# A threshold-attention and SwiGLU kernel: six staging buffers for the gate and value weights, another cutting of the score bursts, and a new written order

## The chip, the cores and the metric

The kernel runs on one core of a Trainium2 chip. Its five engines are TensorE (PE, matmuls, with weight loads listed as PEld), VectorE (DVE), ScalarE (ACT), GpSimd (POOL) and SyncE (SP, which here only issues DMAs). The metric is the time of one execution on the device in microseconds (us), as the median of a few runs. One execution was taken with the hardware profiler; the rows quoted here come from it.

## What is computed

The inputs are q, k and v of shape (8 batches, 8 heads, 576 positions, 64), in fp32. First comes an attention that keeps only scores near the row's maximum, then a feed-forward layer with a gate:

```
scores = (1/8) * q @ k^T                       # per batch and head, 576 x 576
keep   = scores >= max(scores, row) - tau      # tau = 0.02
attn   = softmax(where(keep, scores, -1e9)) @ v
x      = attn, heads side by side              # 4608 tokens x 512
xn     = x / sqrt(mean(x*x) + 1e-6) * rms_g
g      = xn @ w_gate                           # 512 x 1536
val    = xn @ w_val                            # 512 x 1536
out    = (g * sigmoid(g) * val) @ w_out        # 1536 x 512, fp32
```

The scores are computed in fp32. The softmax weights, v, xn and the feed-forward weights are used in fp16.

## The kernel before

**Steps.** The 4608 tokens are 36 chunks of 128 rows: four "m" chunks for each batch, and one "v" chunk for each two batches, made of the last 64 rows of both. A chunk has four steps, one for each pair of heads, so there are 144 steps. A step goes through these stages:

- TensorE computes the scores of the step for both heads of a pair (letter S), fp32, into PSUM banks 0, 1, 3 and 4. One S is a *burst*, and `CHOP` (line 1300) says how many steps are in it: kind 'w' is one step in two half-step parts; a number is a count of columns, so 1024 is 1.78 steps of 576 columns and 1536 is 2.67. A burst may begin only when VectorE has read the banks that it writes.
- VectorE reads the scores, scales them by -1/8, copies them into one of three SBUF buffers `ssb` and takes the row's extreme on the way (`ttr`, letter r, line 767). A step that a burst's end cuts is read in two pieces for each head.
- GpSimd adds tau (`nthr`, letter n), which gives the threshold `nth`.
- ScalarE masks with a Prelu of slope 1e30 (letter p, once for each head) and takes exp of both heads (letter x) into `wsb`.
- The weights are transposed: for the first 16 steps on TensorE (letter T) with an evacuation by VectorE, later by a DMA issued on SyncE (letter t on SP).
- TensorE multiplies by v (letter A, once for two steps), and VectorE divides by the sum (letter h).

When a chunk is complete it is squared and summed (ScalarE, S), its factor is made on GpSimd (m), it is scaled to fp16 (GpSimd, N) and transposed into `xnT`.

**Feed-forward.** Two groups of 256 tokens and eight of 512 each go through 12 column blocks of 128: TensorE's gate product G and value product V (each four matmuls), a tanh on ScalarE (t), then on VectorE `silu` (s) and `gate` (g), which leaves an fp16 block in `hf`. There are 24 such blocks. Twelve of them are tiles of their own, and twelve lie in the memory of `stg`, the staging buffer of the weights. The output product O takes six blocks at a time; ScalarE or VectorE moves its result into `osb` and a DMA stores it. The last group is streamed: its output products follow block by block.

**Weights.** `w_gate` and `w_val` come as twelve loads of 512 KB on SyncE's queue (letter i), each into one of `NSTAGE` = 3 fp32 buffers in turn (line 1217), and GpSimd scales each half by rms_g and casts it to fp16 (letter c, 24 casts, line 1229). A load into a buffer waits for the casts out of it. The third buffer first holds rows of q for the first batch. A `gate` that writes one of the twelve blocks in `stg` for the first time waits for all casts (line 1098). `w_out` comes by four DMAs on GpSimd's queue (M).

**Inputs of later batches.** Batches 0 and 1 load q and k (letters d, D, M, m for batch 0, L for batch 1) and are transposed on TensorE (t, q); later ones are loaded in blocks (l), GpSimd swaps half blocks in place (s) and VectorE transposes (t, T, u). v is loaded (O, a, A) and cast on GpSimd (r).

**Order.** What an engine does, and in which order, is written in `ORDER` (lines 43 to 79): one text for each engine, one letter for each operation; for TensorE the digits after a letter are the PSUM banks that it takes. `in_order` (line 127) reads the texts; each engine then works strictly in its order. `COST`, `DMA_NS`, the due times (`prio`) and the gates belong to the planner that made the texts; here they set no order. What does act on the kernel are the texts, `CHOP`, the buffers and the waits that follow from them.

Of the kernel before, what the change touches and what calls it, by code (L numbers as in the profile page):

```python
# [10 lines left out]
FP16 = mybir.dt.float16  # L11
# [3 lines left out]
AX = mybir.AxisListType  # L15

COST = dict(
    s_main=965.0, s_virt=960.0, tr_qk=570.0, tr4=230.0, tr_full=440.0, av_main=300.0, av_virt=370.0, ffn4=215.8, warm=3500.0,
    evac_qk=600.0, evac_qk_act=465.0, evac_half=252.0, evac_kt=330.0, evac_kt_act=252.0, prelu=667.0, exp2=1060.0, exp1=666.0, exp0=590.0,
    mask_d=680.0, mask_g=1810.0, take_g=1420.0, pool_shift=780.0, pool_sq=1280.0, pool_sum=850.0, trw=510.0, evac_w=400.0, evac_wp=900.0, rz=210.0, xmul=341.0, sq=612.0, xn=773.0,  # L20
    pool_tiny=302.0, pool_mean=944.0, pool_dma=880.0, cast_v=620.0, cast_vt=475.0, cast_w=665.0,
    sp=420.0, sp_v=600.0, sp_w=600.0, sp_tr=1300.0, sp_qk=680.0, sp_tl=630.0, sp_qb=600.0, swap=790.0, turn=600.0, turn_t=210.0, turn_q=680.0,
)
DMA_NS = dict(qkb=1750.0, qk=1200.0, tl=600.0, v=870.0, vt=700.0, wt=1700.0, xt=800.0, out=600.0, w=875.0, wo=2000.0)

LETTERS = dict(
    PE={"emit_av/fn": "A", "emit_burst/fn": "S", "emit_ffn/gmm": "G", "emit_ffn/omm": "O", "emit_ffn/vmm": "V",
# [14 lines left out]
)  # L42
ORDER = dict(
    PE=(
        "wt.1:0t3t1t.1:7St6t7St2t5t6ST67t2t5ST65t7Sq67A2T75ST72SA6q72ST65T72SA2T67ST67q25SA6T72ST67x2Sq62A7x5ST75T62ST67A2k5ST67G2V6G7A1V2T65ST67G0V2",
        "G5SV6G7A5V2SG6V2G5V7G6V2Sl67G2V5A6G7SV2G6V5G1O7V6Sx6A0Ox3O6OA7SG6V7G0V3G1V4A6G7V6SG6V7G0V6G3V7G1V2G4V5G6V7SA6G0V3G1V7A4A6SO6A0OSO7OA2SG6A0V7",
        "G3V1G6A2V7SG6V0G3V1G4V6A7A2SG6V7A0O6SG7V0G3A1O.1:7V2SG0V3G1V4G2V5SOA0A3OA5SO6OSG6V0G7V3G1V4G6V2G0V7G5V6SA7A6A0G3V7O6OSG6V0G3A1V4O7A6SG6V0G3",
        "V1A6G4V2A6SOO6OA5SG6V0G3V1G4V6A7SA6G7V0G3V1G4V6A7SG6O7V0OSG6V0O7A3G4A2OSV6G7A0V3G1V6G4V7A2SO6OO7SA6G0V3OG1V4G6V7A2SG6V0A3O7G3V1G4V6A2SOG0V3",
        "O6A7SG7V0G3A7OV1O7SG6V0G3V1A4G6V2A5SOO6OSG6V0G3V1G4V6A2A7SG7V0A3G1V6G4V7A2SO6G0OV5SG6V0A3G1O7A4V6SG6V0G3V1G4V6OSA6O7OA6SO6A0A3OSG7V0G6V3G7V1",
        "G6V4G2V7G5V6SO7G0A3A1A4V2OSG6V0G3O7V1A6SG6V0G3OV1G4V6A2SA6O7OSG6V0G3V1A4G7V6A2SG7V0G3A6O7OSV6G7V0A3G2O1V3G0V6G4OV7G2V0A3G6A7O3V7A6G2OV0O6OO0",  # L50
        "OG3V1G7V4G3V7G2V3G6V2G7V6G5V1O0G3OO7V5G6OO0134V6G2V5OG2OV6G5OOOOV6OOOOOOOOOOOOOOOOO",
    ),
    ACT=(
        "lT.1TT.2TT.1TppTTxTppxppTTxVppxppppxxVppSxppxppxppVxSppppxxpVpxppxpptExtppxSttppxptpxSptpxttppxvtvpptxttppxppxppxppSxppxpptttxptpppxStxtptpp",
        "ttptxppxxtpptxppSxppxppSxppxpppxpxptpxptpxtSppxptppxttpxppSxtppxppppxxtptppxSpxppxtptptxppxppxSpppxpxppxppppxttxSptpttpptxxtppppxxpSptxptpxp",
        "SpxpptxtppptpxxSppxppppxxtSptpptxpxpptxtptppxSpxtppppxpxpxtptppxpSxppptxttpSxppxpppxpxppptxptxSptpxppptpxtptxpxSpptxppxpptpStxpxppxpptxptptp",
        "xSpxppxppppxtxptptppxxptpSxtptpSpxpxpptppxpxpxtptSppxpxpptxtptpxppxppxSppxppxpppSpxpptxpttxtpptxptxpptpppxxpSxtptppSpxxptpptpxtpxSpxpppppxxp",
        "txtpppxtpxStptppxpppxSxpptpxpptpxxttttSSttttttttttttteses",
    ),
    DVE=(  # L60
        "zcR.1RRrrCrrRRrrSRSrrSSrrhSSrrVSSrrhVrrSSSSrrhSSrrSSVrrhSSrrxSSrrhxVrrSSSSrrSShrSSrsvghSSsgrrrsrSsgSrrrrrrshggrrrsgrrrssggrrrrsghrsr.1rsrsgg",
        "grrxTrrehxrrtTethrrrrrrssgsghgsrgru.2u.2rrrsrgrrssggssggusturrrgrhssghrrtrrhrgrTrThrrrrrrrrrheert.1rrrshgrsrghusrurrrrrsggrrssghht.1grrrrsrr",
        "htgTuurrrrsTrgshrgtrrrTrrrrsTrsggsgrrrrrhrhehrrrerrrerrrrrrssrggsrgsstgsggrrrTrhthrrsThueurrrrsghgsTgrrhrrrrrrsrgshrgshgtrrTrrrruehterrurrss",
        "ggsrrgrrhrrrhsrgstgsrrghrrrrrsrguerrtrrrshrgsuherTrtrrrgrsTgrThsrshggrrrrrruerrrthrTsegrusgrhsrgrrrrhrsrgsgsrghrrrrersrgtthTrrrsrhgrsrgTeurr",
        "rrrsrgrsrghshgTrrrrrertuuerrrrsrgsTgtsrhhrurrrrghrssrgsrhgrrrrrrsggertrrrrhssghrtrgrrrrrsurgssgergrrrhrTrruhTtrrrrhherrurrerurstrsTrgrTrsgss",
        "ggsgrrrrrrhhhsggrerrrssgrgrrhrrrrsrsggrsrgherrrrrrehrrrrsrghsrghrsrrrgsrsrghrrerrrrrgrhsgssgsgghsheshggsegsgssegsgsggessesgggssggessggeeE",
    ),
    POOL=(
        "SnnnrrrrnnrnrcncccnmncccncNcncmncNcrnccncMnrrMncrccrccmncMncNnscnsssncMsrmnsNsnsssssnsssnsssnmsNnsssnssnmnnnnrr.2NnnmnNrnmsNnnsssssnrnssssns",
        "ssssnmrnsrNsssnssnsmnsNnsnnnnmr.1nNnnmnNr.1nnrrnssnsrsnssrmsssnsssnr.1NsssnssnmNsnsr.1ssnnsmsnsNnmNnnnnsrrnsssssnnrmNsssnsnssnmsnNrnssssssns",  # L70
        "r.1nmNnsmsNsnnsr.1nnrrnnnnmsNrsnrsnsssmnssNsnssr.1nr.1msssnsnNsssnssssmNnsnnsnnnmnnNsrnnsssnssmsNnrsrnmsssnsNnsnsssrssnsssnsmnssNnnnmnr.1nnn",
        "r.1NrrnmNnnnnmrNrnmNnnnnnmnnnNnmnNnmNmN",
    ),
    SP=(
        "MmMmdOdDdDDAOLDLSLOOLiOiiLiLiLLiioOOo.1oiiAiOililttllttlltltltAtaasstataTttttttTtllttTtlTltltslttltlttttaTttstttAataTtattTTsltltAtllltsltttl",
        "TtlttstaatsTttTtTtaallttlttltsltltstATlltttTtTstatTtasattsatsltltttllTttAlltsTttllttTtstTatttaslttlaatllttTstllAttltTlsttTtttaTsttstttattTst",
        "atTatttTttsTttsttstttttttTtsTsTTsssssss",
    ),
)

# [93 lines left out]
def kernel(  # L174
# [25 lines left out]
    def sb(name, shape, dt=FP32):  # L200
        return konst.tile(shape, dt, tag=name, name=name)
# [8 lines left out]
    wo = sb("wo", [128, NFC, DM], FP16)  # L210
# [40 lines left out]
    NT_ = 3  # L251
    th = [sb(f"th{i}", [128, 512]) for i in range(NT_)]
    sl = [sb(f"sl{i}", [128, 512]) for i in range(NT_)]
    stg = sb("stg", [128, NSTAGE * 1024])
    stage = [stg[:, 1024 * i:1024 * (i + 1)].rearrange("p (e n) -> p e n", e=2) for i in range(NSTAGE)]
    hf = [sb(f"hf{i}", [128, 512], FP16) for i in range(12)]
    hf += [stg.bitcast(FP16)[:, 512 * i:512 * (i + 1)] for i in range(NHF - 12)]
    osb = [sb(f"osb{i}", [128, DM]) for i in range(2)]
    osb += [ssb[i % NSB][:, i // NSB, 0:DM] for i in range(4)]

# [443 lines left out]
    def emit_burst(segs, prio, runs):  # L704
# [10 lines left out]
        for run in runs:  # L715
            def fn(o, run=run):
                for s, lo, hi, at in run:
                    _, whole, quads = info[s]
                    p = steps[s][1]
                    for rows, bb, lhs in quads if no_whole or o.quad else whole:  # L720
                        for h in range(2):
                            hs = HALF[h]
                            nc.tensor.matmul(bank[rows, at[h]:at[h] + hi[h] - lo[h]], lhs(hs), k_of(bb, p, h)[hs, lo[h]:hi[h]],
                                             start=True, stop=True)

            n = sum(hi[0] - lo[0] for _, lo, hi, _ in run)
            met = [b for s, lo, hi, at in run for h in range(2) for b in banks(at[h], hi[h] - lo[h]) if b not in first]
            for b in met:
                first[b] = lead
            lead += 9.0 + per_col * n  # L730
            made.append(add("PE", 9.0 + per_col * n, prio if not made else -600.0, deps + made[-1:], fn, mode=2 if no_whole else 1))
            made[-1].touches = sorted(set(met))
        made[0].claims = sorted((b, 0.0 if TILE else x) for b, x in first.items())
        writers = {}
# [23 lines left out]
        for n_, (s, lo, hi, at) in enumerate(segs):  # L758
# [7 lines left out]
            for h in range(2):  # L766
# [6 lines left out]

                before = [] if head else [ttr_of[s, h]]
                need = max(writers[b] for b in banks(at[h], hi - lo))
                t = ttr_of[s, h] = add("DVE", 75.0 + (hi - lo) / 0.96, s - 1 + TTR_EARLY + 0.001 * h, (made if TILE else made[:need + 1]) + [o_c, held] + before, ttr)
                t.long = len(segs) > 1 and sum(hi_ - lo_ for _, lo_, hi_, _ in segs) > LONG
                t.reads = list(banks(at[h], hi - lo))
                t.opens = [b for b, last in last_use.items() if (last[1] == h and n_ == len(segs) - 1 if TILE else last == (n_, h))]

    stage_use = []
    ssb_user = {}
    last_burst = []

# [261 lines left out]
    def emit_ffn(slot, parts, ready_step, pace, streamed):  # L1046
# [12 lines left out]
        for fc in range(NFC):  # L1059
# [35 lines left out]
            t = add("ACT", n / 1.2 + 49.0, pr - PUSH[0], [g, th_use.get(i)], tanh, src=(g, 0))  # L1095
            s_ = add("DVE", el, pr - push1, [t, sl_use.get(i)], silu, frees=(g, 0))
            th_use[i] = s_
            m_ = add("DVE", el, pr - push1, [s_, vv] + (stage_use if hi >= 12 and hi not in hf_use else []), gate, frees=(vv, 0))
            sl_use[i] = m_
            hs.append((hi, m_))  # L1100
            uses += [g, vv]
# [112 lines left out]
    for c in range(DFF // 512):  # L1214
        for d in range(0, 4, 2):
            for w_dram, w_sb in ((moe_w_gate, wg), (moe_w_val, wv)):
                slot = n // 2 % len(stage)
                pr = W_FROM + W_STEP * n

                def load(o, d=d, w_dram=w_dram, c=c, slot=slot):  # L1220
# [6 lines left out]
                for e in range(2):  # L1227
# [4 lines left out]

                    ca = add("POOL", COST["cast_w"], pr + W_STEP * e, [lo, o_g], cast)
                    w_use[slot].append(ca)
                    stage_use.append(ca)
                    w_done[c].append(ca)
                n += 2
    wo_ld = []
# [54 lines left out]


PACE = 16.0
GATE = 0.0
SQ_DVE = (0,)
OUT_DVE = (1,)
LAGS = ()
CHOP = ((0, 16, 'w'), (16, 24, 1024), (24, 144, 1536))  # L1300
LONG = 1024
TILE = False
TTR_EARLY = 1.0
# [19 lines left out]
PUSH = (40.0, 0.0)  # L1323
EPUSH = (0, 0.0)
V_AFTER = (2, 0, 0, 0)
B1_BASE = 0.0
WO_AT = 0.0
AV_PRIO = 2.5
HALF_PRIO = 1.2
WAYS = ("pp",)  # L1330
NSTAGE = 3
N_W = 3
NZ = 1
SQ_POOL = 99
# [9 lines left out]
LAT_QB = 4000.0  # L1344
LAT_V = 3500.0
LAT_W = 2400.0
W_FROM = 2.0
W_STEP = 0.4
N_XPE = 4
SOON = (0, 0.0)  # L1350
N_PE = 16
# [40 lines left out]
```

## Time and profile before

| what | value |
|---|---|
| median of 3 runs | 535.59 us (532.46 to 536.45) |
| the profiled execution | 533.01 us |
| its span, first to last instruction | 531.2 us |
| instructions | 14520 |
| TensorE busy | 510.2 us (96%) |
| weight loads busy | 264.9 us (50%) |
| VectorE busy | 458.2 us (86%) |
| ScalarE busy | 442.4 us (83%) |
| GpSimd busy | 223.7 us (42%) |
| DMA | 88.52 MB, mean 167 GB/s |
| TensorE clock granted | full in every slice |

Busy time is the union of an engine's records. Nearly all of the kernel's operations are recorded under one line, L98, since a helper issues them; so a row is told by what it writes and reads (`th<-bank` is the tanh, `bank<-xnT,wg` a gate product, `bank<-qkt` a burst). In the timeline a line gives start, length, engine, line, operation, shapes and count; in brackets stands how long the engine was idle before it and what ended that.

### The profile page before, as it was taken

What the parts mean: (1) busy time and instruction counts of PE and PEld (TensorE: products, weight loads), DVE (VectorE), ACT (ScalarE), POOL (GpSimd) and SP (SyncE); (2) the same over time, 40 slices, a digit from 0 to 9 for tenths busy, and PEclk for the clock granted to TensorE, in tenths of its full rate; (3) what the DMA queues carried; (4) which work ended last, traced back from release to release, by engine and by line L of the source; (5) the groups of instructions that cost most, each with busy time, mean ns of one, the idle gap of its engine ahead of it and who ended that gap; (6) DMA issues with size and microseconds to landing.
All of it is one profiled execution on the core that took longest, in us unless ns stands there. A gap on an engine that the chain in (4) does not pass through costs nothing.

```text
span 531.2 us, 14520 instructions
## 1 busy us (share of the span) xinstructions
PE 510.2 (96%) x5384; PEld 264.9 (50%) x5384; DVE 458.2 (86%) x1260; ACT 442.4 (83%) x648; POOL 223.7 (42%) x478
## 2 busy tenths in 40 slices
PE   7888999999999999999999999999999999999995
PEld 4556565554544545545454545454454554454442
DVE  4899998998999889999998989999999888864652
ACT  5899899999999987998899889989998889871310
POOL 0367787236841366517653277326651321202000
PEclk9999999999999999999999999999999999999999
DMA  8999999999977999999899999798979769563112
GB/s 180 255 250 260 205 170 227 197 156 213 176 132 142 190 207 167 180 177 195 173 158 196 173 194 181 148 227 185 182 143 155 121 127 156 97 127 83 41 39 80
DMA packets 218887, 88.52 MB, mean 167 GB/s; under 512 B 195264, under 2 KB 204992, under 8 KB 218816
## 3 DMA queue, kind: packets, MB, share of 16 engines
q1 hardware_dynamic: 216016, 85.49, 82.2%
q0 software_dynamic: 1600, 1.57, 2.2%
q8 instruction: 42, 0.69, 0.5%
q10 hardware_dynamic: 1200, 0.52, 0.3%
q14 instruction: 29, 0.24, 0.2%
HBM read 37.75 MB, written 9.44 MB: 89 GB/s over the span
## 4 chain that ended last, share of the span: by engine, by line
PE 56%; DVE 12%; ACT 5%; issue 4%; DMA 2%; POOL 1%; SPq 0%; POOLq 0%; DVEq 0%; ACTq 0%
PE bank L98 56%; DVE ssb L98 5%; ACT ssb L98 3%; DVE sl L98 2%; ACT wsb L98 2%; DVE qkt L98 1%; DMA qkx<-in_k_dram 1%; DVE hf L98 1%; DMA vst<-in_v_dram 1%; DVE stg L98 1%; DVE xsb L98 1%; POOL spare L98 1%; POOL qkx L98 0%; DVE mx L98 0%; DVE osb L98 0%
## 5 line engine op out<-in xcount | busy, mean ns | idle before, releaser
L98 ACT ACTIVATE ssb<-ssb,nth 128x576 f32<-128x576 f32 x288 | 209.4, 766 | 12.5 <-POOL nth L98 12.3
L98 DVE CUSTOM_DVE_ANT_0 ssb<-bank,zcol 128x576 f32<-128x576 f32 (+3 forms) x288 | 185.6, 679 | 20.9 <-PE bank L98 14.8
L98 ACT ACTIVATE wsb<-ssb 128x1152 f16<-128x1152 f32 x144 | 165.4, 1158 | 3.1 <-DMA wt<-wsb 1.3
L98 PE MATMUL bank<-qkt 64*64 64x64 f32 (+8 forms) x2272 | 156.2, 410 | 6.0 <-DVE mx L98 3.5
L98 PE MATMUL bank<-xnT,wg 128*128 128x512 f16 (+1 forms) x480 | 113.3, 359 | 2.1 <-DVE mx L98 1.8
L98 PE MATMUL bank<-xnT,wv 128*128 128x512 f16 (+1 forms) x480 | 113.1, 358 | 1.4 <-DVE xsb L98 0.6
L98 POOL TENSOR_SCALAR nth<-mx 128x2 f32<-128x2 f32 x144 | 30.9, 214 | 188.3 <-DVE mx L98 177.8
L98 ACT ACTIVATE th<-bank 128x512 f32<-128x512 f32 (+1 forms) x120 | 64.8, 546 | 49.2 <-PE bank L98 45.1
L98 PEld LDWEIGHTS bank<-qkt 64*64 64x64 f32 x2272 | 72.0, 133 | 65.8 <-issue 23.4
L98 DVE SCALAR_TENSOR_TENSOR sl<-th,bank 128x512 f32<-128x512 f32 (+1 forms) x120 | 74.3, 627 | 19.2 <-ACT th L98 18.7
L98 PEld LDWEIGHTS <-wv 128*128 128x128 f16 x480 | 44.9, 98 | 51.6 <-DVE mx L98 6.1
L98 PEld LDWEIGHTS <-wg 128*128 128x128 f16 x480 | 42.6, 98 | 55.0 <-issue 7.0
L98 PEld LDWEIGHTS <-wt 128*128 128x128 f16 (+1 forms) x1440 | 50.1, 100 | 18.9 <-DVE mx L98 3.3
L98 PE MATMUL bank<-va,wt 128*128 128x65 f16 (+3 forms) x1440 | 54.1, 196 | 0.5 <-DVE wt L98 0.3
L98 PE MATMUL bank<-wo,hf 128*128 128x512 f16 x216 | 50.9, 379 | 0.5 <-ACT ssb L98 0.5
L98 PE MATMUL bank<-wo,stg 128*128 128x512 f16 x216 | 50.9, 379 | 0.4 <-DVE xsb L98 0.4
L98 DVE STREAM_TRANSPOSE qkt<-qkx 128x128 f32<-128x128 f32 (+2 forms) x72 | 41.7, 588 | 0.0
L98 DVE TENSOR_TENSOR stg<-bank,sl 128x512 f16<-128x512 f32 (+1 forms) x60 | 37.0, 630 | 2.8 <-PE bank L98 2.4
L98 DVE CUSTOM_DVE_ANT_0 ssb<-bank,zcol,mxp 128x384 f32<-128x384 f32 (+4 forms) x68 | 32.9, 513 | 5.1 <-PE bank L98 4.1
L98 DVE TENSOR_TENSOR hf<-bank,sl 128x512 f16<-128x512 f32 (+1 forms) x60 | 36.9, 629 | 0.4
L98 POOL COPY spare<-qkx 32x576 f32<-32x576 f32 x48 | 31.6, 657 | 7.1 <-DMA qkx<-in_k_dram 4.5
L98 DVE TENSOR_TENSOR xsb<-bank,rz 128x256 f32<-128x256 f32 x72 | 30.6, 425 | 4.4
(45 smaller groups left out, 372.7 us busy)
## 6 DMA issues: line engine op xcount, KB each, us to landing
vst<-in_v_dram SPq DMA_DIRECT2D x32, 256.0 KB, 4.3
qkx<-in_k_dram SPq DMA_DIRECT2D x24, 288.0 KB, 3.7
qkx<-in_q_dram SPq DMA_DIRECT2D x24, 288.0 KB, 3.8
out_dram<-osb SPq DMA_DIRECT2D x48, 128.0 KB, 2.6
stg<-in_moe_w_gate_dram SPq DMA_DIRECT2D x6, 512.0 KB, 5.7
stg<-in_moe_w_val_dram SPq DMA_DIRECT2D x6, 512.0 KB, 5.3
wt<-wsb SPq DMA_TRANSPOSE x128, 3.7
out_dram<-osb SPq DMA_DIRECT2D x8, 256.0 KB, 3.2
```

Of the source, the lines that this page charges most:

```text
L98: made = got(*args, **kw)
```

## The change

Six things change.

- The staging tile `stg` is twice as large and holds all 24 feed-forward blocks; the twelve tiles `hf0` to `hf11` are gone, so the memory is the same. It gives six fp32 buffers. The twelve weight loads take them in the order `W_SLOTS`; buffers 3, 4 and 5, which are blocks 0 to 11, are used once each, by the third, fourth and fifth load.
- The first write of each of blocks 0 to 11 now waits for the casts out of buffers 3 to 5, that of blocks 12 to 23 for the casts out of buffers 0 to 2.
- Steps 8 to 15 go in bursts of 1024 columns, as steps 16 to 23 did; steps 0 to 7 remain single.
- The written orders of all five engines are new.
- Constants of the planner change (`COST`, `DMA_NS`, `GATE`, `B1_BASE`, `W_FROM`, `W_STEP`, the costs of bursts and reductions).
- Twelve load and cast letters (i, c) stay as many as before; the reductions r become 364 instead of 356, and the bursts S 62 instead of 66. All other letters keep their counts.

```diff
 ORDER = dict(
     PE=(
-        "wt.1:0t3t1t.1:7St6t7St2t5t6ST67t2t5ST65t7Sq67A2T75ST72SA6q72ST65T72SA2T67ST67q25SA6T72ST67x2Sq62A7x5ST75T62ST67A2k5ST67G2V6G7A1V2T65ST67G0V2",
-        "G5SV6G7A5V2SG6V2G5V7G6V2Sl67G2V5A6G7SV2G6V5G1O7V6Sx6A0Ox3O6OA7SG6V7G0V3G1V4A6G7V6SG6V7G0V6G3V7G1V2G4V5G6V7SA6G0V3G1V7A4A6SO6A0OSO7OA2SG6A0V7",
...
+        "wt.1:0t3t7t.1:2St6t7t2St6t5t7ST67t1St5T62ST67q25SA6T72SA6q72ST65T72ST67A2T65x7Sq67A5T72Sq67T25T72Sk6T72A5x6ST67A2T65SG6T72A5T72SV7G5A2V6G7S",
+        "l67V2G5V6G7A2Sx5V6G7V2G5V7G6A2SV6G7V0G3O6V4A7SG7V0G3V1x4A7SO.1:7G0OV3G1A2OA5SV6G7V0G3V1G6A4V7G2V5G6SA6V0G7V3G6V1G4V2G5V7G6SV6O7A0G3OV6SO6A3",
...
     POOL=(
-        "SnnnrrrrnnrnrcncccnmncccncNcncmncNcrnccncMnrrMncrccrccmncMncNnscnsssncMsrmnsNsnsssssnsssnsssnmsNnsssnssnmnnnnrr.2NnnmnNrnmsNnnsssssnrnssssns",
...
+        "SnnnrrrrrnnnrccnrnmNcnccccnccnccMcnMmncNncnc.1MncrrcnnrsncccnsrmcncNrnsssmnMNnccsnssssnmsnssnsnsssssssnsssNnnnnmNnmNnmNnrr.2sssnsnsr.2r.2rsn",
...
     SP=(
-        "MmMmdOdDdDDAOLDLSLOOLiOiiLiLiLLiioOOo.1oiiAiOililttllttlltltltAtaasstataTttttttTtllttTtlTltltslttltlttttaTttstttAataTtattTTsltltAtllltsltttl",
...
+        "mMmMdddDDDALODOOLoLSALOOiiio.1iiLLLiLiiOillioiOttlOtltittltltllttttatatastTtTttllAaTsTttllttlltttAlstlTtttTtaatattttsTattTtllstltlstAlttlttT",
...
-    stg = sb("stg", [128, NSTAGE * 1024])
-    stage = [stg[:, 1024 * i:1024 * (i + 1)].rearrange("p (e n) -> p e n", e=2) for i in range(NSTAGE)]
-    hf = [sb(f"hf{i}", [128, 512], FP16) for i in range(12)]
-    hf += [stg.bitcast(FP16)[:, 512 * i:512 * (i + 1)] for i in range(NHF - 12)]
+    stg = sb("stg", [128, 2 * NSTAGE * 1024])
+    stage = [stg[:, 1024 * i:1024 * (i + 1)].rearrange("p (e n) -> p e n", e=2) for i in range(2 * NSTAGE)]
+    hf = [stg.bitcast(FP16)[:, 512 * i:512 * (i + 1)] for i in list(range(12, 24)) + list(range(12))]
...
-            m_ = add("DVE", el, pr - push1, [s_, vv] + (stage_use if hi >= 12 and hi not in hf_use else []), gate, frees=(vv, 0))
+            m_ = add("DVE", el, pr - push1, [s_, vv] + ([] if hi in hf_use else stage_use if hi >= 12 else first_use), gate, frees=(vv, 0))
...
-                slot = n // 2 % len(stage)
+                slot = W_SLOTS[n // 2]
...
-                    stage_use.append(ca)
+                    (first_use if slot >= NSTAGE else stage_use).append(ca)
...
-CHOP = ((0, 16, 'w'), (16, 24, 1024), (24, 144, 1536))
+CHOP = ((0, 8, 'w'), (8, 24, 1024), (24, 144, 1536))
...
+W_SLOTS = (0, 1, 3, 4, 5, 2, 0, 1, 2, 0, 1, 2)
```

## The prediction

> **What bounds the kernel now.** I read the page's first part, then busy time by stage, then the intervals between starts in TensorE's timeline, and last what ScalarE waited for. The stages below end where a burst of score matmuls starts: the bursts of steps 4, 16, 24, 42.7 and 61.3 (found in the timeline at 19.27, 56.65, 79.64, 135.92 and 196.74), then the last exponential at 472.
>
> ```profile
> 0.00:19.27 19.27, 14.67 (x126) 8.28 (x126) 11.30 (x36) 11.43 (x22) 3.57 (x14) 1.00 0.89 184
> 19.27:56.65 37.38, 32.04 (x513) 22.11 (x512) 33.75 (x95) 36.23 (x51) 21.18 (x42) 1.00 1.00 258
> 56.65:79.64 22.99, 22.27 (x253) 13.81 (x252) 21.63 (x76) 19.99 (x35) 19.21 (x36) 1.00 1.01 190
> 79.64:135.92 56.28, 54.01 (x683) 30.29 (x682) 52.41 (x161) 54.76 (x82) 29.22 (x63) 1.00 1.07 202
> 135.92:196.74 60.82, 58.85 (x588) 28.32 (x587) 56.23 (x157) 57.95 (x85) 28.29 (x62) 1.00 0.91 168
> 196.74:472.00 275.26, 274.87 (x2937) 137.32 (x2937) 253.55 (x689) 248.66 (x354) 119.36 (x259) 1.00 0.88 165
> ...
> 490.00:500.00 10.00, 10.00 (x48) 4.49 (x46) 7.48 (x12) 3.58 (x6) 0.00 (x0) 1.00 0.12 27
> ```
>
> After the window and its length the columns are TensorE, its weight loads, VectorE, ScalarE and GpSimd busy, then clock, DMA share and GB/s. ScalarE is the limit from step 4 to 16 (36.23 of 37.38 us); between 56.65 and 136 three engines share it; later TensorE has no visible gap. Is it then really full? Its records overlap, so I take starts:
>
> ```profile
> 190.60 1.03 PE L98 MATMUL bank<-xnT,wv 128*128 128x512 f16 x4
> 191.47 1.03 PE L98 MATMUL bank<-xnT,wg 128*128 128x512 f16 x4
> 192.33 1.03 PE L98 MATMUL bank<-xnT,wv 128*128 128x512 f16 x4
> ...
> 196.74 2.82 PE L98 MATMUL bank<-qkt 64*64 64x384 f32 x40
> 199.49 2.19 PE L98 MATMUL bank<-va,wt 128*64 128x130 f16 x90
> 201.79 1.04 PE L98 MATMUL bank<-xnT,wg 128*128 128x512 f16 x4
> ```
>
> Four matmuls of 512 columns take 0.866 us from start to start, a 1536-column burst 2.75 us (196.74 to 199.49), an output part of six 1.30. Setting every group of TensorE against the shortest interval of its kind leaves, as lost time, 4.2 to 5.0 us in each 20 up to 60 us, 3.1, 2.4 and 1.8 in the next three, 4 in all from 136 to 197, and some 4 us in the 275 after it. From 197 us on TensorE is packed, and no order can give much there.
>
> [...] Weight loads fill 137.32 of 275.26 us: by that share half of TensorE is free, and an order that keeps ScalarE from waiting would shorten the run. But in 490 to 500 us, where 48 matmuls of 0.21 us leave no room at all, the same share is 4.49 of 10. So here neither share tells a full engine from a half full one, and the intervals decide. By the share the new order could gain the 6.8 us of ScalarE's two large stalls (below); by the intervals nothing. I take nothing.
>
> **The change, part by part.** The order is written out, so I count letters between bursts (G gate, V value, O output part, A attention times V, S a burst).
>
> *Feed-forward starts later.* At the burst of step 24 the old order has issued 12 G, 12 V, 1 O; the new one 8, 7, 0. At 42.7 both have 27, 27, 8. So 4 G, 5 V (256 columns, 0.44 us each from the timeline's 101.67, 102.12) and one O (1.30), 5.3 us of TensorE, move from before 79.64 to the stage after it; with them 4 tanh (0.27 each between starts, 1.1) on ScalarE and 8 to 9 VectorE operations of 256 columns (0.33 of interval, 2.7).
>
> *Bursts of 1.78 steps from step 8.* Eight half-step pairs become 4.5 bursts. Cutting a step of 576 columns into 384 and 192 replaces 751 by 612 + 348 ns and one accumulator read of 84 more: 0.29 us. The order has 364 reductions where it had 356, so VectorE gains 8 x 0.29 = 2.3 us. TensorE needs 1.13 us a step in the old form (12.87 to 14.00) against 1.03 in the large bursts: at most 0.8 us less, where it isn't the limit: 0. Fewer, larger hand-overs could help only if the engines waited on them; ScalarE idles 1.15 us in the whole stage of steps 4 to 16.
>
> *Stage 19.27 to 79.64 (60.37 us).* ScalarE 36.23 + 19.99 - 1.1 = 55.1. VectorE 33.75 + 21.63 - 2.7 + 2.3 = 55.0. The first part ran at 97% of ScalarE; with VectorE as full I take 96%: 57.4, so -3.0. Bounds: -4.5 (no idle beyond 1%), and 0, where the cuts and the hand-over of 1.78 steps at once use up what the tanh leave.
>
> *Stage 79.64 to 135.92 (56.28 us).* TensorE's own need was 56.3 less 4.9 lost = 51.4; with 5.3 it is 56.7. ScalarE is 55.9, VectorE 55.4. Three engines within 2%: at the 94% of the stage 135.92 to 196.74 it lasts 60.3, at the 98% of the later ones 57.8. I take 59.0: +2.7. The cover for the moved work was TensorE's idle; it is gone, and the next thing late is TensorE itself.
>
> *First 19.27 us.* On the load queue the key loads of pairs 2 and 3 move ahead of the first value load (0.69 us), that of pair 3 of a query load too (1.90). The value loads fall back, that of pair 1 from 12.22 to about 16 us; it lands in 4.3 and is cast in 0.63, so at 21. Its user, the first attention product, starts at 20.9 now and stands one burst (2.9 us) later in the new order: 0. ScalarE waits 1.41 us at 19.38 for a transpose that was behind VectorE's evacuation of the banks, and 0.45 at 11.76. The key-tail load goes ahead of the first query load (0.5 us later; TensorE is in its warm-up until 4.6, which hides it). Bounds -2 to +0.5; I take -1.0.
>
> *Six buffers.*
>
> ```profile
> 21.99 0.47 SPq L98 DMA_DIRECT2D stg<-in_moe_w_gate_dram  x1
> 22.50 0.66 SPq L98 DMA_DIRECT2D qkx<-in_k_dram  x1
> 29.09 0.37 SPq L98 DMA_DIRECT2D stg<-in_moe_w_val_dram  x1
> ```
>
> The fourth weight load waits 5.9 us for a cast, with a query load queued behind it. With six buffers the first six loads need no cast. But TensorE never waits for a weight, and GpSimd for weights only 0.87 and 0.74 us, so the gain is 0. [...] By the rows, TensorE's waits for key loads are 1.1 us in all. The order puts four of the eight loads ahead of all weights; I take 0, bounds 0 and +6.1. The new wait, of the first 12 gated blocks on the casts out of the upper buffers, has the later gated blocks and reductions of VectorE queued behind it; those casts are done by the 11th threshold, some six steps before the first gate: 0. Putting all blocks in one memory: today's stg and hf forms take 630 and 629 ns with 2.8 and 0.4 us of idle, so 0, at most +2.4. The last cast moves from the 21st to the 24th threshold, one step ahead of its user in both orders: 0 to +0.9. Block loads and half-swaps keep about four steps between them in both; one pair of batch 3 has two: 0 to +1.6, the wait of 1.58 seen at 187.83.
>
> *After 135.92.* Same work, another order. The old one issues six G-V pairs in a row before the bursts of steps 61.3 and 125.3; the new one splits both into three and three.
>
> ```profile
> 202.86 0.60 ACT L98 ACTIVATE th<-bank 128x512 f32<-128x512 f32 x1 [3.99 <-PE bank L98]
> ...
> 399.47 126.00 PE bank L98 x1018
> ```
>
> (ScalarE's timeline, then a piece of the chain that ended last.) These lumps cost ScalarE 3.99 us at 202.86 and 2.8 between 412 and 423, but TensorE worked through both: its part of the chain from 399 us is one unbroken piece. I take 0, bounds -4 (all that TensorE still loses from 136 on, half of it) and +5 (1.5% of 336 us, the loss of a worse order).
>
> **Sum.** -1.0 - 3.0 + 2.7 = -1.3 us against the profiled 533.01 (span 531.2): 531.7. The median of the three runs is 2.6 above that execution, so 535.6 - 1.3 = 534.3.
>
> **Rivals.** *Faster, 528:* the stalls of ScalarE do count, since TensorE's loss before 197 us hangs on how early softmax results come: -1.3 and the 6.8 of the two lumps give 527.5, a part of it 528 to 530. For it: ScalarE's waits; against: that unbroken piece. 0.27. *Slower, 542:* the debt. The 5.3 us that leave the first stage don't quicken it, because VectorE, with 2.3 us more, takes over from ScalarE; and the next stage pays in full, 60.3. Then 0 + 4.0 + 2.3 = +6.3: 541.9. It decides if the burst of step 24 starts later than about 79 us. 0.17. *Weights in the way, 539:* half of the 6.1 us with the bound +1.6: about 538 to 541. 0.07. *My forecast*, 530.5 to 538: 0.49.
>
> **Numbers.** Three runs spread by 0.75%, so 1% is about what can be told from no change. Under 530.2: the faster rival's 0.22 and 0.05 of mine, 0.27. Over 540.9: 0.17 and a part of the weights and of a worse late order, 0.22. Range 527 to 541.5: it leaves out the far half of the two outer rivals, about 2 in 10.
>
> **What would show it.** Right: step 24's burst starts at 75 to 77 us, that of 42.7 at 134 to 136; ScalarE's waits at 203 and 412 us are gone and the time from 136 us to the end is within 2 us of 395. Wrong: TensorE idle over 1 us in the later stages, waits for stg loads over 2 us, or an end that moves with ScalarE's stalls.

## The result, and the profile after

The changed kernel takes 535.04 us, the median of 22 runs (533.57 to 538.17). The kernel before takes 533.27 (22 runs, 532.46 to 536.45). The ratio is 1.0031, with a 95% interval of 1.0019 to 1.0043. The change makes the kernel slower by 1.7 us in 534, where a gain of 1.3 was forecast. The 535.59 us of before was the median of three runs; 22 runs, those three among them, put it 2.3 lower. So the predicted 534.3 us lies near the measured 535.04 only because its basis was too high. The profiled executions, 533.01 and 534.71 us, differ by the same 1.7, and they can be set against each other stage by stage.

The busy time by stage after the change, with the same columns (window and length, TensorE, its weight loads, VectorE, ScalarE, GpSimd, clock, DMA share, GB/s), and the stages cut at the same steps (16.9 for 16):

```profile
0.00:19.48 19.48, 14.69 (x126) 7.90 (x126) 10.60 (x34) 11.85 (x24) 2.85 (x13) 1.00 0.88 194
19.48:58.21 38.73, 30.64 (x446) 21.62 (x444) 33.51 (x107) 33.63 (x47) 21.58 (x43) 0.96 0.98 248
58.21:79.53 21.32, 19.68 (x268) 13.66 (x266) 20.67 (x75) 21.14 (x36) 15.15 (x30) 1.00 0.85 169
79.53:139.43 59.90, 59.07 (x724) 34.02 (x721) 57.40 (x174) 57.81 (x90) 36.33 (x74) 1.00 1.09 199
139.43:197.49 58.06, 56.27 (x632) 28.78 (x629) 54.30 (x150) 53.66 (x78) 26.93 (x58) 1.00 0.96 171
197.49:472.00 274.51, 272.81 (x2873) 136.90 (x2868) 253.07 (x690) 250.13 (x353) 117.74 (x256) 1.00 0.86 164
490.00:500.00 10.00, 10.00 (x48) 4.51 (x46) 5.06 (x8) 1.95 (x4) 0.00 (x0) 1.00 0.27 60
```

In the second row no engine is full: ScalarE works 33.63 of 38.73 us, where it was the limit before, and the clock has fallen to 0.96. Set side by side:

| stage | before | forecast | after |
|---|---|---|---|
| start to step 4's burst | 19.27 | 18.3 | 19.48 |
| to step 24's burst | 60.37 | 57.4 | 60.05 |
| to step 42.7's burst | 56.28 | 59.0 | 59.90 |
| to the end | 395.28 | 395.3 | 393.47 |

The gain of the second stage, 3.0 us in the forecast, is missing. The rows of that stage show where it goes. First SyncE's queue: five weight loads are issued from 24.06 to 28.5 us, where the kernel before issued three from 20.21 to 22.5 and the fourth at 29.09.

```profile
24.06 0.47 SPq L99 DMA_DIRECT2D stg<-in_moe_w_gate_dram  x1
...
25.60 0.61 SPq L99 DMA_DIRECT2D qkx<-in_k_dram  x1
26.25 1.75 SPq L99 DMA_DIRECT2D stg<-in_moe_w_val_dram  x1
...
29.81 4.36 SPq L99 DMA_DIRECT2D qkx<-in_q_dram  x1
34.27 3.40 SPq L99 DMA_DIRECT2D qkx<-in_k_dram  x1
37.72 0.89 SPq L99 DMA_DIRECT2D stg<-in_moe_w_val_dram  x1
```

In the kernel before, the first of them stood here:

```profile
20.21 0.69 SPq L98 DMA_DIRECT2D stg<-in_moe_w_gate_dram  x1
```

The first weight is now issued 3.9 us later. Two cast letters stand directly behind each other on GpSimd's queue and wait for it. GpSimd's timeline:

```profile
26.47 0.62 POOL L99 TENSOR_SCALAR va<-vst 128x512 f16<-128x512 f32 x1 [0.99 <-DMA vst<-in_v_dram]
30.61 1.36 POOL L99 TENSOR_SCALAR wg<-stg,rmsg 128x512 f16<-128x512 f32 x2 [3.52 <-DMA stg<-in_moe_w_gate_dram]
32.06 0.21 POOL L99 TENSOR_SCALAR nth<-mx 128x2 f32<-128x2 f32 x1
```

The threshold at 32.06 took 0.21 us and waited for nothing of its own. It stood behind the casts. The next engines in the chain are ScalarE, then TensorE:

```profile
32.31 0.78 ACT L99 ACTIVATE ssb<-ssb,nth 128x576 f32<-128x576 f32 x1 [2.60 <-POOL nth L99]
```

```profile
31.05 1.96 PE L99 MATMUL bank<-qkt 64*64 64x512 f32 x24 [0.59 <-DVE mx L99]
36.13 1.14 PE L99 MATMUL bank<-id,wsb 128*128 128x128 f16 x9 [3.12 <-ACT wsb L99]
37.07 1.30 PE L99 MATMUL bank<-va,wt 128*128 128x130 f16 x18
```

Before the change GpSimd waited 0.87 us for that first weight, with one cast between two thresholds, and ScalarE did not wait here at all:

```profile
26.87 0.69 POOL L98 TENSOR_SCALAR wg<-stg,rmsg 128x512 f16<-128x512 f32 x1 [0.87 <-DMA stg<-in_moe_w_gate_dram]
28.07 0.21 POOL L98 TENSOR_SCALAR nth<-mx 128x2 f32<-128x2 f32 x1 [0.50 <-DVE rz L98]
```

The nine transposes at 36.13 in the changed kernel need 0.94 us to the next start instead of 0.61 (nine others, 43.50 to 44.11). The windows around the pause (same columns as above) show why:

```profile
33.00:36.00 3.00, 0.01 (x2) 0.00 (x0) 1.44 (x4) 3.00 (x7) 2.25 (x5) 0.98 1.09 319
36.00:37.00 1.00, 0.87 (x9) 0.87 (x10) 0.00 (x0) 0.97 (x3) 0.83 (x3) 0.50 1.30 239
37.00:38.00 1.00, 1.00 (x18) 1.00 (x17) 0.69 (x2) 1.00 (x2) 1.00 (x3) 0.50 0.70 125
38.00:39.00 1.00, 1.00 (x15) 1.00 (x13) 1.00 (x4) 1.00 (x2) 1.00 (x2) 0.50 0.42 94
39.00:40.00 1.00, 1.00 (x14) 0.90 (x13) 0.59 (x4) 0.97 (x2) 0.16 (x1) 0.86 1.37 247
```

Near the end of the pause of 3.12 us the granted clock falls to 0.50, and it stays there for 3.4 us (35.86 to 39.22). In the profile of the kernel before it is 1.00 in all rows of this stage.

The bursts of steps 24 and 42.7 came later than the prediction's signs allow. Its other two signs came out nearly as it said: ScalarE's long wait at 203 us is gone (the tanh at 202.82 follows its neighbour without a wait), that at 412 fell from 1.96 to 0.81 us at 414, and from step 42.7 to the end it took 393.47 us. From 183 us on the chain is nearly all TensorE:

```profile
202.82 0.57 ACT L99 ACTIVATE th<-bank 128x512 f32<-128x512 f32 x1
```

```profile
182.70 168.21 PE bank L99 x1794
351.88 110.55 PE bank L99 x1157
...
467.83 59.62 PE bank L99 x336
```

(ScalarE's timeline, then three pieces of the chain that ended last: start, length and number of matmuls.) So there is little room to win back what is lost early. Two signs of being wrong appeared as well. GpSimd's wait of 3.52 us for a weight is over the 2 us named, and TensorE waits for VectorE 1.44 us at 154.16 and 1.64 us at 467.83, where its longest wait from 136 us on was 0.68 us before:

```profile
467.83 1.04 PE L99 MATMUL bank<-xnT,wg 128*128 128x512 f16 x4 [1.64 <-DVE mx L99]
```

### The profile page after: what moved, and what is told of

Read it like the earlier page. It is cut to its first block, busy times and chain, and to the rows that moved or that the text cites. A ratio compares the mean times of both kernels' runs of the same rounds, so it can differ in the third digit from the quotient of the medians.

```text
span 532.9 us, 14451 instructions
## 1 busy us (share of the span) xinstructions
PE 508.6 (95%) x5352; PEld 268.7 (50%) x5352; DVE 459.7 (86%) x1276; ACT 443.8 (83%) x648; POOL 224.1 (42%) x478
## 3 DMA queue, kind: packets, MB, share of 16 engines
q0 software_dynamic: 1600, 1.57, 2.0%
## 4 chain that ended last, share of the span: by engine, by line
PE 73%; DVE 15%; DMA 3%; issue 3%; ACT 2%; POOL 2%; SPq 1%; DVEq 0%; POOLq 0%
PE bank L99 73%; DVE ssb L99 8%; DMA vst<-in_v_dram 2%; DVE stg L99 2%; DVE qkt L99 1%; DVE sl L99 1%; SPq L99 1%; ACT ssb L99 1%; DMA xnT<-xn 1%; DVE xsb L99 1%; DVE wt L99 1%; DMA stg<-in_q_dram 1%; POOL qkx L99 1%; ACT wsb L99 0%; ACT qkt L99 0%
## 5 line engine op out<-in xcount | busy, mean ns | idle before, releaser
L99 DVE CUSTOM_DVE_ANT_0 ssb<-bank,zcol 128x576 f32<-128x576 f32 (+5 forms) x288 | 183.3, 671 | 16.9 <-PE bank L99 13.7
L99 PE MATMUL bank<-qkt 64*64 64x448 f32 (+10 forms) x2240 | 155.0, 410 | 5.1 <-DVE mx L99 4.2
L99 PEld LDWEIGHTS bank<-qkt 64*64 64x64 f32 (+1 forms) x2240 | 73.3, 134 | 62.2 <-issue 22.6
L99 PE MATMUL bank<-wo,stg 128*128 128x512 f16 x432 | 101.8, 379 | 0.1
L99 DVE TENSOR_TENSOR stg<-bank,sl 128x512 f16<-128x512 f32 (+1 forms) x120 | 73.7, 628 | 3.0 <-PE bank L99 1.9
L99 PEld LDWEIGHTS <-stg 128*128 128x128 f16 x432 | 40.6, 98 | 54.0 <-issue 3.8
L99 PEld LDWEIGHTS <-wt 128*128 128x128 f16 (+1 forms) x1440 | 51.7, 100 | 18.0 <-issue 3.0
L99 PE MATMUL bank<-va,wt 128*128 128x65 f16 (+3 forms) x1440 | 55.5, 197 | 0.3 <-POOL va L99 0.2
L99 DVE CUSTOM_DVE_ANT_0 ssb<-bank,zcol,mxp 128x384 f32<-128x384 f32 (+7 forms) x76 | 36.2, 510 | 3.4 <-issue 2.4
L99 POOL COPY qkx<-spare 32x576 f32<-32x576 f32 x48 | 31.7, 660 | 3.0
```

What stands on the lines that cost most here:

```text
L99: made = got(*args, **kw)
```

## The experiments

**The theory** after the first comparison: the forecast's gain is lost in the first 60 us, and the loss comes from two casts that stand on GpSimd's queue ahead of thresholds that are ready, while their weight is still on its way; the low clock adds to it. **Rivals:** the six buffers themselves; the coarser bursts of steps 8 to 15; the later order; too many weight bytes ahead of the key and query loads; the low clock alone.

### Which half, and the buffers

The changed kernel's orders up to about step 72, then those of before. (The orders are long; these two diffs, and those of GpSimd's and SyncE's queue below, are abridged.)

```diff
-ORDER = changed kernel's texts
+ORDER = changed kernel's texts up to the cut, then the texts of before
```

> The changed kernel up to about step 72, and from there the orders of the kernel before (all engines' orders are cut where both have done the same work). Theory (all of the loss lies before step 42.7, and from there both orders keep TensorE full): within 1 us of the changed kernel, 534.5 to 536, ratio 1.002 to 1.005. Rival (the late order matters, ScalarE's stalls in it too): the old late order alone brings the time near that of before, 533.5 or less, or adds over 1 us.

Measured: 536.55 us, ratio 1.0051 (1.0038 to 1.0064), above the 534.5 to 536 of the theory: the loss is there, and a further one.

The reverse, with the three buffers of before:

```diff
-ORDER = texts of before
+ORDER = texts of before up to the cut, then the changed kernel's texts
```

> The kernel before up to about step 72 (its three weight buffers, its early orders), the changed kernel's orders from there on. If the loss of the change lies in its first 60 us and its later order is itself a small gain, this keeps the gain without the loss: 531.5 to 532.8 us, a ratio of 0.997 to 0.999, with the burst of step 42.7 at 136 us as before. If the later order is worth nothing, 533.3 and a ratio of 1.000; if it is what costs, 534.5 or more.

Measured: 534.26 us, ratio 1.0023 (1.0010 to 1.0035); the burst of step 42.7 starts at 135.43 us. For a later order that gains, 531.5 to 532.8 was expected.

The two halves do not add up: 0.51% and 0.23% against 0.31% for the whole change. A seam can have a price of its own, since neither text was made to follow the other. Between the bursts of steps 72 and 141.3 the kernels need 228.93 us (before), 228.73 (after) and 228.95 (the reverse splice), so the late orders are worth the same to 0.1%. In the reverse splice the burst at the seam stops in its middle for VectorE and takes 3.66 us to the next start, where the kernel before needs 2.75 (224.29 to 227.04):

```profile
223.99 1.85 PE L99 MATMUL bank<-qkt 64*64 64x384 f32 x24
226.51 1.21 PE L99 MATMUL bank<-qkt 64*64 64x64 f32 x16 [0.67 <-DVE mxp L99]
227.65 4.06 PE L99 MATMUL bank<-wo,stg 128*128 128x512 f16 x18
```

The expected early loss is there; that the later order is a gain of its own was not shown. The first splice is 1.1 us slower (by the ratios) than the whole change. Its profile, at 534.37 us the fastest of its 22 runs, does not show where, so that stays open; a seam is the likely cause.

Only the buffers, with all orders of before:

```diff
-    stg = sb("stg", [128, NSTAGE * 1024])
+    stg = sb("stg", [128, 2 * NSTAGE * 1024])
...
-                slot = n // 2 % len(stage)
+                slot = W_SLOTS[n // 2]
```

> The kernel before with the six staging buffers, their slot order and their waits alone; its written orders and bursts stay, so the fourth to sixth weight loads go out up to 6 us sooner. Theory: nothing waits for a weight in that kernel, the buffers by themselves are worth 0: 533.3, ratio 0.998 to 1.002. Rival (weights crowd out the query and key loads): up to 6 us later loads of the second batch, ratio 1.003 to 1.010. Rival (buffers are a gain that the new orders lose): ratio under 0.997.

Measured: 533.32 us, ratio 0.9990 (0.9977 to 1.0003). Six buffers and one memory cost nothing and bring nothing while the order stays.

### What stands in GpSimd's queue

The two casts go behind two thresholds and a cast of v. The letters are n threshold, r cast of v, c cast of a weight, m and N the norm:

```diff
-POOL  SnnnrrrrrnnnrccnrnmN
+POOL  SnnnrrrrrnnnrnrnccmN
```

> The changed kernel, with the first two weight casts moved two thresholds later in GpSimd's order (SnnnrrrrrnnnrccnrnmN becomes SnnnrrrrrnnnrnrnccmN); nothing else. Theory (head of GpSimd's queue): the loss before step 16.9 comes from those casts, which wait 3.5 us for a weight load with two finished steps' thresholds behind them; ScalarE's waits of 2.60 us at 32 and 1.74 at 42 and TensorE's pause of 3.1 us go, its clock stays full, and the time falls by 3 to 5 us against the changed kernel: 530 to 532, ratio to the kernel before 0.994 to 0.998. Rival (bursts of 1.78 steps stand behind the transposes of steps 7 and 8 and come too late whatever GpSimd does): ScalarE's wait at 32 shrinks but that at 42 and a TensorE pause of over 2 us stay; 534 to 535, ratio 1.001 to 1.004.

Measured: 532.71 us, ratio 0.9986 (0.9973 to 0.9998). Two letters moved take 2.3 us off the changed kernel's 535.04, less than the 3 to 5 expected, and make it as fast as before or a little faster. The coarser bursts are in this run too, so they are not what cost those 2.3 us. Its profiled execution, at 534.15 us one of its slowest, has no wait at 32 us any more (the threshold at 31.00 waits for VectorE, the casts at 31.30 for nothing), and ScalarE runs 2.5 us ahead of the changed kernel near 45 us:

```profile
31.00 0.21 POOL L99 TENSOR_SCALAR nth<-mx 128x2 f32<-128x2 f32 x1 [1.38 <-DVE mx L99]
31.30 1.36 POOL L99 TENSOR_SCALAR wg<-stg,rmsg 128x512 f16<-128x512 f32 x2
```

But step 24's burst is at 79.52 there too: the lead is gone by 50.7. This execution has a low clock at another place. TensorE's timeline:

```profile
47.05 3.74 PE L99 MATMUL bank<-qkt 64*128 64x384 f32 x16
50.63 0.41 PE L99 MATMUL bank<-id,qkx 64*128 64x64 f32 x4
```

That burst takes 3.58 us to the next start; in the changed kernel the same one takes 1.90. The clock from 47.24 to 50.60 was 0.51. Ahead of it GpSimd had waited 2.49 us at 43.76 for the sixth weight and TensorE 0.88 at 44.71 for a query load.

The opposite remedy, the first three weights to the front of the load queue (i weight, O and A value, L key or query):

```diff
-SP    LSALOOiii
+SP    LSiiiALOO
```

> The changed kernel, with the first three weight loads moved ahead of the value loads of batches 0 and 1 (LSALOOiii becomes LSiiiALOO on SyncE's queue), so that they are issued about 4 us sooner; GpSimd's order stays. Theory (head of GpSimd's queue): the load lands before the casts come up, the wait of 3.5 us goes, 530 to 532.5, ratio 0.994 to 0.999, unless the value loads that now stand behind make a wait of their own. Rival (late bursts): 534 to 535. Rival (the load engines are full, share 0.9 to 1.1, so what goes first only moves the wait): a wait for vst or qkx of 1.5 us or more in its place, 534 to 537.

Measured: 539.09 us (538.09 to 539.82), ratio 1.0095 (1.0067 to 1.0124). The wait moved to the loads that were pushed back, and grew:

```profile
33.22 0.62 POOL L99 TENSOR_SCALAR va<-vst 128x512 f16<-128x512 f32 x1 [6.65 <-DMA vst<-in_v_dram]
```

In this execution the clock was also low, 0.76 in the mean from 31 to 45 us. So this load is not early for free, and what a queue runs in order has to be asked on both sides: what arrives when, and what stands behind it.

### The order of the loads

With the casts moved as above, the sixth weight load goes ahead of three key and query loads (o is the load of the key tails):

```diff
-SP    LSALOOiiio.1iiLLLiLi
+SP    LSALOOiiio.1iiiLLLLi
```

> The changed kernel with the first casts behind two thresholds (as in the run cast_later) and, in addition, the sixth weight load issued ahead of the three key and query loads that stand blocked on the load queue from 30 to 37 us. If the stage from step 8 to 17 is held up by what stands in GpSimd's and the load queue's order, GpSimd's wait of 2.49 us at 43.76 goes, the burst of step 16.9 moves from 58.2 to 56 to 57 us and the time falls to 530.5 to 531.8 (0.995 to 0.997). If ScalarE and VectorE bound that stage whatever the order of casts, the time stays at cast_later's 532.7. If 0.52 MB more ahead of the key and query loads hurts, TensorE's waits for qkx loads grow and it is 533 to 535.

Measured: 533.91 us, ratio 1.0017 (1.0003 to 1.0031). GpSimd's wait at 43.76 is gone, and TensorE pays for it:

```profile
40.06 0.46 PE L99 MATMUL bank<-id,qkx 64*128 64x64 f32 x8 [2.22 <-DMA qkx<-in_k_dram]
...
43.18 3.33 PE L99 MATMUL bank<-qkt 64*128 64x256 f32 x16
46.34 0.66 PE L99 MATMUL bank<-id,qkx 64*128 64x64 f32 x16
```

Against the run with the casts moved alone, the key load's wait grew from 0.62 to 2.22 us, and the burst after it needs 3.16 us instead of 1.83, at a clock of 0.50 from 43 to 45 us.

The same load between the two blocked ones:

```diff
-SP    LSALOOiiio.1iiLLLiLi
+SP    LSALOOiiio.1iiLLiLLi
```

> As the run load6, but the sixth weight load goes between the two blocked key and query loads (issue at about 34 us instead of 28.3 or 37.4). If the order of weights against key loads is what matters, TensorE's wait for the key load stays at 0.6 us (2.2 in load6), GpSimd's wait of 2.49 us for the last weight is under 1 us, and the time is 531 to 532.3. If 0.52 MB ahead of any key load costs TensorE as much as it spares GpSimd, 532.7 to 534.

Measured: 532.42 us, ratio 0.9973 (0.9958 to 0.9988). TensorE waits 0.79 us for the key load, GpSimd still 1.65 for the weight (under 1 was expected), and step 24's burst starts at 78.26.

Weights and key or query loads in turn:

```diff
-SP    LSALOOiiio.1iiLLLiLi
+SP    LSALOOiiio.1iLiLiLLi
```

> As load6_between, with the fifth weight load also behind the key load it now precedes, so that weights and key or query loads alternate. Same bytes, another order: if key and query loads are held up by the weights ahead of them on the 16 shared DMA engines, TensorE's waits for qkx loads from 38 to 45 us (0.62, 0.63 and 0.88 in cast_later) shrink to under 1 us in all and the time is 530.8 to 532. If the total of bytes and not the order sets it, the waits move to GpSimd's casts and the time is 532.5 to 534.

Measured: 532.39 us (531.32 to 533.68), ratio 0.9980 (0.9970 to 0.9990). TensorE waits for none of these loads from 38 to 45 us, and from 30 to 70 us no cast waits for a weight. The windows of its stages:

```profile
19.57:55.74 36.17, 29.71 (x447) 20.36 (x445) 33.52 (x107) 33.75 (x47) 21.52 (x43) 1.00 1.04 266
55.74:77.06 21.32, 19.68 (x269) 13.65 (x267) 20.67 (x75) 21.14 (x36) 15.15 (x30) 1.00 0.86 183
77.06:136.95 59.89, 59.12 (x723) 34.01 (x721) 57.41 (x174) 57.79 (x90) 36.32 (x74) 1.00 1.08 195
```

The same work as in the changed kernel (33.52 and 33.75 us on VectorE and ScalarE, against 33.51 and 33.63) now takes 36.17 instead of 38.73 us, at a full clock. The two stages after it are the same to 0.01 us (21.32, and 59.89 against 59.90), and the end comes 2.4 us sooner (span 530.5 against 532.9). This and the run before it are faster than both kernels. But their intervals overlap with that of the casts moved alone (0.9973 to 0.9998), so a gain of the order of the loads is not shown in the medians; what is shown is that in this profile the waits named above are gone.

Was it the loads alone? The same order of loads with the casts where the change put them:

> The changed kernel with the alternating order of weight and key or query loads of the run loads_spread alone: the first two casts stay ahead of the two thresholds. If the place of the casts on GpSimd's queue is the main loss, ScalarE's wait of about 2.6 us near 32 us and the pause of TensorE after it stay, and the time is 534 to 535.2 (1.001 to 1.0035). If the load order was the whole of it, 532.4 as loads_spread.

Measured: 535.28 us (534.06 to 537.18), ratio 1.0037 (1.0023 to 1.0050).

```profile
32.03 1.37 POOL L99 TENSOR_SCALAR wg<-stg,rmsg 128x512 f16<-128x512 f32 x2 [4.40 <-DMA stg<-in_moe_w_gate_dram]
```

```profile
33.73 0.78 ACT L99 ACTIVATE ssb<-ssb,nth 128x576 f32<-128x576 f32 x1 [3.30 <-POOL nth L99]
```

```profile
37.56 0.68 PE L99 MATMUL bank<-id,wsb 128*128 128x128 f16 x9 [3.94 <-ACT wsb L99]
```

(GpSimd, ScalarE and TensorE of that run.) This profiled execution is the slowest of its 12 runs, so its waits are on the long side. But the whole chain of the changed kernel is back, and the median with it: with the casts ahead of the thresholds the ratio is 1.0031 and 1.0037 for the two orders of loads, with the casts behind them 0.9986 and 0.9980. The place of two casts on GpSimd's queue is the main loss, and the order of the loads alone wins nothing.

### The price of the low clock

The changed kernel with needless matmuls in the pause; the results are the same:

```diff
             def tr(o):
+                for _ in range(42 if s == 6 else 0):
+                    nc.tensor.matmul(ring[o.slot[0]][:, 0:128], id16, id16, start=True, stop=True)
                 for j in range(9):
```

> The changed kernel with 42 needless 128-column matmuls (about 2.8 us) at the head of the ninth-step transposes that wait at 33 to 36 us; the results are the same. If the low clock after the pause costs time by itself, the clock stays at 1.00 from 33 to 42 us, the transposes at 36 us take 0.6 us instead of 0.94, and the time falls by 1 to 1.5 us to about 533.8 (1.0005 of before). If the clock costs nothing because TensorE is not what the stage waits for, 535.0 as for the changed kernel (1.003); if the matmuls themselves delay the transposes, 535.5 or more.

Measured: 533.73 us (14 runs), ratio 1.0011 (0.9998 to 1.0023), where the changed kernel had 1.0031 (1.0019 to 1.0043). The median clock of the runs is 0.999 against 0.995. That is a fall of about 1.1 us, where 1 to 1.5 was expected, but the two intervals overlap a little. The profiled execution cannot show the gain, because it lost as much elsewhere: TensorE waited 1.57 us for a query load before 18.79, the clock was 0.50 from 20 to 22 us, and the burst of step 8 came at 32.83 instead of 31.05. With less pause left, the added matmuls delayed the transposes.

The first splice gives a second figure. Its profile has the same early orders and nearly the same pause, and there the clock stayed at 1.00 from 31 to 45 us:

```profile
36.28 0.68 PE L98 MATMUL bank<-id,wsb 128*128 128x128 f16 x9 [2.90 <-ACT wsb L98]
```

From the burst of step 8 to that of step 24 it needs 47.56 us (31.43 to 78.99), the changed kernel 48.48 (31.05 to 79.53). Of these 0.9 us the shorter pause is 0.2, so I estimate the low clock's price at 0.7 to 1.1 us. It adds to the loss and is not the whole of it.

The same against the low clock near 47 us, in the version with the casts moved:

```diff
             for j in (1, 0):
+                for _ in range({2: 8, 3: 14}.get(n, 0) if j == 0 else 0):
+                    nc.tensor.matmul(ring[o.slot[0]][:, 256:384], id16, id16, start=True, stop=True)
                 for c in range(4):
```

> The run cast_later with 8 and 14 needless 128-column matmuls inside two transposes that wait for query loads at 39.8 and 44.7 us; the results are the same. In cast_later's profile the burst at 47.05 us ran at a clock of 0.50 to 0.57 and took 3.58 us to the next start where the changed kernel's took 1.90. If that low clock is what eats the lead of 2.5 us, the clock stays at 1.00 from 43 to 52 us, the burst of step 24 starts at 77.5 to 78 instead of 79.52, and the median is 531.5 to 532.3 (0.996 to 0.998). If the stage ends at 79.5 whatever the clock, 532.7 as cast_later.

Measured: 533.07 us, ratio 0.9992 (0.9979 to 1.0005); 531.5 to 532.3 was expected. In the profiled execution the clock is 1.00 from 43 to 53 us and step 24's burst starts at 76.93, 2.6 us sooner than in the profile of the version without. But the median is not below its 532.71. The low clock near 47 us seems not to be in every execution of that version: by my estimate (3.4 us at 0.50 in the profiled span of 532.4 us) one such stretch takes 0.003 off an execution's mean clock, and nine of its 22 executions have 0.998 or more. The seven at 0.996 or less, the profiled one among them, take 533.67 us in the median, the other fifteen 532.35. So, by this estimate, only some 0.4 us of the median was there to win. That the added matmuls cost about as much in each execution is argued, not shown.

## Why the prediction was wrong, point by point

**The step that failed** is that of the six buffers: "TensorE never waits for a weight, and GpSimd for weights only 0.87 and 0.74 us, so the gain is 0", with the value 0 taken. These waits belonged to the old order, with the first weight issued at 20.21 us and one cast between two thresholds. The prediction's part on the first 19.27 us saw that loads change places, but the step on the buffers did not carry that to the weights, nor ask what is queued behind a cast. The new orders put two casts ahead of thresholds and their load 3.9 us later. What the runs showed in place of the 0 is a loss: moving the two casts alone wins back 2.3 us of the median, and the burst of step 24 comes at 79.53 us in the changed kernel, at 77.06 with casts and loads in place, 2.5 us apart. The buffers as such were rightly put at 0 (the run with the buffers only, ratio 0.9990).

**The stage of steps 4 to 24** (-3.0 to 57.4 us; 60.05 measured) failed with it. Its arithmetic was right: with casts and loads in place the stage takes 57.49 us. There ScalarE works 54.89 of the 57.49 us, 95%, where 96% was assumed; in the changed kernel it works 54.77 of 60.05, 91%, with waits for thresholds of 2.60 and 1.74 us among its gaps.

**The fourth case, weights in the way**, had 0.07. One such delay was measured: with 0.52 MB more ahead of the key loads one wait grew from 0.62 to 2.22 us. But the loss in the changed kernel was mainly another: thresholds held up by casts. The bound of 6.1 us for this case was an estimate, 1.57 MB at the 258 GB/s of steps 4 to 16; the longest wait of TensorE for a key or query load in the rows here is 2.22 us.

**The slower rival, the debt**, had the right decision point (the burst of step 24 later than about 79 us) for another reason. VectorE did not take over as the limit: it works 33.51 of 38.73 us. Its added busy time over the kernel is 1.5 us, against 2.3 for the cuts.

**The stage to step 42.7** (+2.7 to 59.0; 59.90 measured) was right in its mechanism: TensorE is busy 59.07 of it, the moved work is paid in full, and it is 59.89 to 60.30 us in the five versions with the casts moved. The size was 0.9 short; the 60.3 of the upper bound was the nearer end.

**The first 19.27 us** (-1.0; +0.2 measured). ScalarE's wait of 1.41 us at 19.38 shrank only to 0.94 at 19.09: the transpose it waits for now waits for the query load that the change pushed back. This is the same omission in small, a load moved ahead of others and the others' users not followed.

```profile
18.53 0.52 PE L99 MATMUL bank<-id,qkx 128*128 128x128 f32 x3 [1.23 <-DMA qkx<-in_q_dram]
```

**After 135.92** (0; -1.8 measured, within the bound of -4). All of it lies between the bursts of steps 42.7 and 72 (95.70 us before, 93.80 after, with the same 21 gate and 21 value products and 12 output parts; one attention product fewer, some 0.6 us, since three of them take 1.79 us from 413.99 us on before). From step 72 to the end the kernels are equal (299.6 and 299.7). That ScalarE's stalls cost nothing late in the run is borne out at 412 us: the first splice keeps that lump, with a wait of 1.96 us at 414, and from step 42.7 to its end it takes 393.7 us against 393.5. How much of the rest comes from splitting the lump at 203 was not tested.

**The sum** with the measured terms is +0.2 - 0.3 + 3.6 - 1.8 = +1.7 us, the measured difference.

## What to carry to other kernels

A wait read in the profile belongs to the order it was measured in: when a change moves a load, or the instruction that uses it, find the new issue and landing times and then name what stands behind that instruction on its engine, above all short instructions that another engine needs at once. Put work whose input may be late behind such instructions, not ahead of them, and only then look at the order of the loads. Where the engine at the end is packed, as TensorE is here from 183 us on, microseconds lost early mostly stay lost: the 2.5 us that the mended orders gain by step 24 are still 2.4 us at the end.

## What the runs showed of the hardware

TensorE's granted clock fell to one half near some of the short pauses. In the profiled executions it was 0.50 for 3.4 us near pauses of 3.12 us (the changed kernel, 35.86 to 39.22), 2.22 (the run with the sixth load in front; 0.75 from 42 to 43 us, 0.50 to 45, 0.54 to 46) and 1.57 (the run with matmuls in the pause; 0.55 from 19 to 20 us, 0.50 to 22, 0.74 to 23), and for some 6.8 us near one of 3.94 us (the order of loads alone; 0.76 from 37 to 40 us, 0.50 to 45, 0.96 to 50). The length of one pause does not decide it: near a pause of 2.90 us in the first splice the clock stayed at 1.00 from 31 to 45 us, and in the run with the casts moved it was 0.51 for 3.4 us after a stretch with no pause above 0.9 us, in which TensorE was busy 2.44 of 4 us (43 to 47). Nor did the low stretch always follow the pause at once: in the run with the sixth load in front it began at about 42.5 us, 2.4 us after work had started again at 40.06. What starts a low stretch and what ends it was not shown.

The time that a DMA issue took on SyncE differed several times over: 4.36 and 3.40 us for the query and key loads at 29.81 and 34.27 in the changed kernel, behind five weight loads and with the DMA share at 1.1, where the query load at 22.15 took 0.62 us with the share at 0.40 from 22 to 23 us. The DMA share alone does not explain it, since in the kernel before an issue at 22.50 took 0.66 us with the share at 1.21 from 22 to 23 us. What these issues stood for was not found.
